# Turning late token tiles in 32 x 32 blocks on VectorE, and making decay weights ahead, in a fused state-space and feed-forward kernel

## The chip, the cores and the metric

The kernel runs on one core of one Trainium2 chip, as one program. The metric is device time in microseconds (us) of one execution. The core has five engines that run side by side, each with a queue of its own that it works through in order: PE (TensorE, matmuls; PEld is its weight loads), DVE (VectorE), ACT (ScalarE), POOL (GpSimd) and SP (SyncE, which here only issues DMAs).

## The reference

Two branches work on the layer-normed input and are added to the input: a diagonal state-space convolution (S4), and a feed-forward with SiLU. Everything is float32.

```python
def _A_ref(u, A_re, A_im, B_re, B_im, C_re, C_im, log_dt, Dskip):   # u: 1 x 2048 x 576
    dt = jnp.exp(log_dt)[:, None]
    A = A_re + 1j * A_im                                             # 576 x 128
    ...
    logdA = dt * A
    dB = dt * Bc
    P = jnp.exp(logdA[:, :, None] * l[None, None, :])                # l = 0 .. 2047
    K = jnp.einsum("dn,dnl,dn->dl", Cc, P, dB).real
    ...                                                              # causal convolution of u with K, by FFT
    y = (lambda x, *d: x.transpose(*d))(y, 0, 2, 1) + u * Dskip[None, None, :]
    return y

def _B_ref(x, w1, w2):                                               # w1: 576 x 4608, w2: 4608 x 576
    h = jnp.einsum("bsd,df->bsf", x, w1)
    h = _silu(h)
    out = jnp.einsum("bsf,fd->bsd", h, w2)
    return out

x = A_u
xn = _layernorm(x, axis=-1)
return x + _A_ref(xn, ...) + _B_ref(xn, B_w1, B_w2)
```

## The kernel before

The 2048 tokens are 16 tiles of 128. A product of two float32 matrices is made of three products of rounded parts: each operand is split into a high part (a copy to the rounded type F32R on ScalarE) and a low part (operand minus high part, on VectorE), and high x high, high x low and low x high are added up in PSUM.

**The feed-forward** (`ffn`) is the main line. It walks over 36 blocks: two halves of the tokens (tiles 0 to 7, 8 to 15), nine chunks of 512 hidden channels, and two blocks of 512 tokens. For a block, `up` multiplies a chunk of w1 with the turned token tiles `xh`, `xl`, `x4` (L284 to L286, 14 matmuls), applies SiLU (L292) and splits the result into `gh` and `gl` (L293, L294); `down` multiplies that with w2 (L309, 12 matmuls for each half of the 576 channels, into one of three `po` accumulators) and adds to the accumulator `acc` in SBUF (L313). `load_w1`, `split_w1`, `load_w2` and `split_w2` bring the next chunk in from SP's queue. The steps of a block are written out by hand as u0, d0 to d3, u1, u2, u3, where the u steps belong to the next block.

**The turned tokens.** The up projection needs tokens with channels on the partitions. `normed` takes normalised tiles from `norm` and turns each on PE in `put_xt`: four 128 x 128 transposes (L121) and one of the last 64 channels (L125) into the PSUM tile `pt`, then a copy on ScalarE (L122, L126) and a subtraction on VectorE (L123, L127), which give the high and low part. Tiles 0 to 7 go straight into `xts[0]` and `xts[1]`. Tiles 8 to 15, the late ones, are not needed before the second half. They go through one buffer `xt` in SBUF and from there to DRAM (`dxt`, L223), nine groups of 128 channels that hold the high parts, the low parts and the last 64 channels' pair. `next_xt` loads them back, as three DMAs on POOL's queue for each block of 512 tokens (L322 to L324), when the first half reaches its last chunk. The normalised tile itself goes to `dxn` (L224) for the convolution.

**The side line** (`side`) is woven into the feed-forward by `weave`, which hands out its pieces at given shares of the main line's steps. In order:
- `phase0` for the first eight tiles, before the main line starts;
- in turn, `natural` (the decay and phase of each of 576 channels x 128 states, first in a layout of 96 x 6 x 128) and `phase0` for the four late pairs. `natural` leaves the exponentials of the decay at lags 256, 64, 8 and 1 in `ex`, which go to DRAM as `dexp` (L436), and turns three arrays on PE with `turned` (L393, L394) into `fT`, `rhoT` and `phiT`, which stay in SBUF;
- `kgen`, which makes the convolution kernel's transform in 36 chunks of 16 channels. For each pair of chunks `powers` loads the four bases (`load_bases`, L519), lays them out in `pw` and makes their powers 0 to 7 (L528, L532 to L534), and multiplies the first four powers at lag 64 with `rhoT` into `al` (L536). A chunk makes phases (`head`, L541, L543; L557, L558), sines and cosines (L559 to L561), magnitudes from products of the powers (L562 for 32 columns, L566 for 64), products of both (L577, L578), many small matmuls into `kp` (L598) and, for each pair, a transform with `f1` (L613), whose result is staged (L621) and written to `d1k` (L626) every two pairs;
- `spread`, the token side of the transform, one piece for each chunk of `kgen` from the third on;
- `spectral`, 32 steps of products in the frequency domain, and `tail`, which turns back and adds to the output.

The order of instructions on each engine is made at build time by a scheduler that simulates the engines and takes, of what is ready, the earliest emitted; `high_priority` puts L292 to L294 and L313 first, and `behind` keeps an instruction behind a given one on its engine. The tile pools `nat` and `pb` (for `natural` and the late pairs) are closed before `kgen` opens its own, in the same memory.

## Time and profile before

| | |
|---|---|
| median of 3 runs | 1133.25 us (1133.01 to 1133.71) |
| the profiled execution | 1131.89 us, its span 1130.1 us |
| PE, PEld busy | 1109.0 us, 999.9 us |
| DVE, ACT, POOL busy | 917.1 us, 709.0 us, 74.3 us |
| DMA | 151.24 MB in 160458 packets, of which 87216 under 512 B |

The profile is of one execution. Its parts are the page (busy time, the span in slices, queues, the chain that ended last, the costliest groups, the DMA issues), groups of instructions by line and operation, windows of time, waits and timelines. A group's line has the count, the busy time and the mean length of one in ns, and the idle time of the engine just before them with what ended it. A line number such as L309 is one of the kernel before. Matmuls overlap, so that the time a matmul holds PE is read from one start to the next and not from its length.

### The profile page before, as it was taken

The page shows a single profiled execution, that of the slowest core. Times are in us where ns is not written, and L with a number is a line of the kernel's source. Part 1 is how long each engine was busy: PE and PEld are TensorE (multiplying, and loading weights), DVE is VectorE, ACT ScalarE, POOL GpSimd, SP SyncE. Part 2 cuts the span into 40 slices and gives each one's busy share as a digit, 9 for nine tenths or more (in the row PEclk, how much of TensorE's full clock was granted, in tenths as well). Part 3 has the DMA queues.
Part 4 walks back from the last instruction along what each step waited for, and adds up shares of the span by engine and source line. Part 5 has one row for each costly group of instructions (what it writes and reads, how often), then busy time and mean ns, then how long its engine had stood idle before and what let it go on. Part 6 is the DMA issues. An engine that isn't in the chain of part 4 may idle for free.

```text
span 1130.1 us, 22882 instructions
## 1 busy us (share of the span) xinstructions
PE 1109.0 (98%) x9184; PEld 999.9 (88%) x9184; DVE 917.1 (81%) x1540; ACT 709.0 (63%) x1235; POOL 74.3 (7%) x130
## 2 busy tenths in 40 slices
PE   6999999999999999999999999999999999999998
PEld 5988889988889888898989999999999999998876
DVE  6699779999999999999999937788877878763433
ACT  4665355776777666667666637877777787752211
POOL 1010000000000000001000000000000000000210
PEclk9999999999999999999999999999999999999999
DMA  9345431334241424255954264554535536239661
GB/s 277 111 142 181 144 96 60 97 98 103 83 114 59 112 83 106 90 127 192 231 161 104 66 183 122 157 175 132 170 114 157 166 118 195 72 111 243 174 171 55
DMA packets 160458, 151.24 MB, mean 134 GB/s; under 512 B 87216, under 2 KB 127168, under 8 KB 159712
## 3 DMA queue, kind: packets, MB, share of 16 engines
q1 hardware_dynamic: 150128, 112.66, 36.2%
q0 software_dynamic: 9840, 36.24, 10.0%
q8 instruction: 72, 1.18, 0.4%
q10 hardware_dynamic: 384, 0.89, 0.3%
q14 instruction: 34, 0.28, 0.1%
HBM read 103.74 MB, written 46.08 MB: 133 GB/s over the span
## 4 chain that ended last, share of the span: by engine, by line
PE 65%; DVE 24%; DMA 5%; ACT 3%; issue 3%; POOL 0%; SPq 0%; DVEq 0%; ACTq 0%; POOLq 0%
PE po L309 28%; PE ph L284 23%; DVE acc L313 2%; DVE C L566 2%; PE pu L721 2%; PE pb L721 2%; PE pk L721 2%; DVE th L541 2%; DMA w2r<-in_B_w_dram 2%; DVE th L558 2%; DVE S L577 2%; PE ph L285 2%; PE ph L286 2%; DVE C L577 2%; DVE gl L294 2%
## 5 line engine op out<-in xcount | busy, mean ns | idle before, releaser
L309 PE MATMUL po<-w2h,gh 128*128 128x288 f32 x1152 | 338.5, 297 | 5.3 <-DVE acc L313 2.6
L309 PE MATMUL po<-w2l,gh 128*128 128x288 f32 x1152 | 337.1, 295 | 0.0
L309 PE MATMUL po<-w2h,gl 128*128 128x288 f32 x1152 | 335.3, 296 | 0.6 <-DVE gl L294 0.6
L309 PEld LDWEIGHTS po<-w2h,gh 128*128 128x128 f32 x1152 | 215.2, 188 | 16.8 <-DVE acc L313 4.9
L309 PEld LDWEIGHTS po<-w2l,gh 128*128 128x128 f32 x1152 | 215.5, 188 | 4.3
L309 PEld LDWEIGHTS po<-w2h,gl 128*128 128x128 f32 x1152 | 214.8, 188 | 3.0 <-issue 0.9
L284 PE MATMUL ph<-xh,w1h 128*128 128x512 f32 (+1 forms) x592 | 162.3, 390 | 0.5 <-ACT xh L122 0.5
L284 PE MATMUL ph<-xl,w1h 128*128 128x512 f32 (+1 forms) x592 | 162.1, 387 | 0.0
L284 PE MATMUL ph<-xh,w1l 128*128 128x512 f32 (+1 forms) x592 | 161.1, 385 | 0.0
L313 DVE TENSOR_TENSOR acc<-po,acc 128x288 f32<-128x288 f32 x288 | 126.9, 452 | 40.1 <-PE po L309 38.4
L292 ACT ACTIVATE gf<-ph 128x512 f32<-128x512 f32 (+1 forms) x148 | 86.6, 585 | 115.3 <-PE ph L286 106.1
L294 DVE TENSOR_TENSOR gl<-gf,gh 128x512 fp32r<-128x512 f32 (+1 forms) x148 | 99.6, 673 | 47.6 <-ACT gh L293 46.9
L284 PEld LDWEIGHTS ph<-xl,w1h 128*128 128x128 f32 x592 | 108.6, 190 | 20.2
L284 PEld LDWEIGHTS ph<-xh,w1l 128*128 128x128 f32 x592 | 108.0, 188 | 19.7
L284 PEld LDWEIGHTS ph<-xh,w1h 128*128 128x128 f32 x592 | 105.3, 190 | 19.0 <-issue 2.3
L293 ACT CAST gh<-gf 128x512 fp32r<-128x512 f32 (+1 forms) x148 | 89.7, 608 | 9.1 <-PE po L309 6.2
L559 ACT ACTIVATE c<-th 128x1040 f32<-128x1040 f32 x36 | 38.7, 1075 | 60.0 <-DVE th L558 59.9
L271 ACT CAST w2h<-w2r 128x576 fp32r<-128x576 f32 x72 | 46.7, 672 | 39.9 <-DMA w2r<-in_B_w_dram 23.4
L557 ACT ACTIVATE c<-th,magic 128x1040 f32<-128x1040 f32 x36 | 42.0, 1168 | 42.4 <-DVE C L578 36.5
L273 DVE TENSOR_TENSOR w2l<-w2r,w2h 128x576 fp32r<-128x576 f32 x72 | 53.4, 752 | 8.9 <-ACT w2h L271 8.9
L286 PE MATMUL ph<-x,w1l 128*128 128x512 f32 (+1 forms) x148 | 56.9, 385 | 0.0
L255 DVE TENSOR_TENSOR w1l<-w1r,w1h 128x640 fp32r<-128x640 f32 x72 | 56.7, 819 | 0.2
(186 smaller groups left out, 1847.2 us busy)
## 6 DMA issues: line engine op xcount, KB each, us to landing
w2r<-in_B_w_dram SPq DMA_DIRECT2D x72, 288.0 KB, 3.7
w1r<-in_B_w_dram SPq DMA_DIRECT2D x35, 512.0 KB, 3.8
d1u<-u POOLq DMA_DIRECT2D x32, 288.0 KB, 2.8
d1k<-stage SPq DMA_DIRECT2D x18, 512.0 KB, 7.2
ur<-d1u SPq DMA_DIRECT2D x32, 288.0 KB, 3.6
kr<-d1k SPq DMA_DIRECT2D x32, 288.0 KB, 2.8
d<-yo POOLq DMA_DIRECT2D x32, 288.0 KB, 3.6
ys<-d SPq DMA_DIRECT2D x32, 288.0 KB, 9.0
```

The costliest lines, as they stand in the source:

```text
L255: pins["w1l"] = nc.vector.tensor_sub(l1, src, h1).ins
L271: pins["w2h"] = nc.scalar.copy(h2, r2).ins
L273: nc.vector.tensor_sub(l2, r2, h2)
L284: nc.tensor.matmul(ph, w[:, kt, :], v[:, kt, a:e], start=n + kt == 0, stop=False)
L286: pins["pe"] = nc.tensor.matmul(ph, l1[:, 4, :], x4[:, a:e], start=False, stop=True).ins
L292: nc.scalar.activation(gf, ph, AF.Silu)
L293: pins["gh"] = nc.scalar.copy(gh, gf).ins
L294: pins["gl"] = nc.vector.tensor_sub(gl, gf, gh).ins
L309: pins["pe"] = nc.tensor.matmul(po[:, :HD], G[blk, t][g][:, js], W2[half, c, t][w][:, hs], start=n == 0, stop=n == 3 * FT - 1).ins
L313: nc.vector.tensor_add(acc[j][:, hs], po[:, :HD], acc[j][:, hs])
L577: nc.vector.tensor_mul(ov3, t[:, :, 0:64].rearrange("n d (x y) -> n d x y", y=32), mv3)
L721: nc.tensor.matmul(dst, st, mv[:, hs], start=n == 0, stop=n == 3 * len(terms) - 1)
```

## The change

The late token tiles are no longer turned on PE. VectorE turns each normalised tile in blocks of 32 x 32 into a tile `tr` (one buffer for a pair of tiles), and eight DMAs for each pair put the blocks in their places in `dxt`, which now holds plain float32 tokens with channels on the rows (576 x 512). `next_xt` loads the first 512 channels into `xl` and the last 64 twice into `r4`, a buffer of the pool's `gl` tag. A new `split_xt` makes the high part (a copy on ScalarE) and the low part (a subtraction in place on VectorE), in five pieces for each of the two late blocks, after steps d3, u1 and u2 of the first half's last chunk.

In the decays, the table of powers keeps three bases (256, 8 and 1). The powers 0 to 3 of the lag-64 base times `rho` are made in `natural` for all channels (`wt`, three multiplications), written to DRAM as `dmag`, and loaded for each pair of chunks into `wb` beside the bases `eb`. `al` and `rhoT` go away. The magnitudes of the first 32 columns are made by two instructions, one for each group of eight channels, in place of one.

```diff
-    dxt = [dram.tile([P, 9, 512], F32, name=f"dxt{b}") for b in range(2)]
+    dxt = [dram.tile([D, 512], F32, name=f"dxt{b}") for b in range(2)]
...
-    dexp = dram.tile([P, 4 * D], F32, name="dexp")
+    dexp = dram.tile([P, D, 3], F32, name="dexp")
+    dmag = dram.tile([P, D, 4], F32, name="dmag")
...
-            else:
-                xt = p0.tile([P, 9, P], F32R, tag="xt", name="xt", bufs=1)
-                put_xt(xt[:, 0:4, :], xt[:, 4:8, :], xt[:, 8, :], xn[:, i, :])
-                nc.sync.dma_start(dxt[b - 2][:, :, jj * P:(jj + 1) * P], xt.bitcast(F32))
+        if js[0] >= 8:
+
+            b, jj = divmod(js[0], 4)
+            tr = p0.tile([P, 2, D], F32, tag="tr", name="tr")
+            for i in range(2):
+                nc.vector.transpose(tr[:, i, :], xn[:, i, :])
+            for q in range(4):
+                cols = dxt[b - 2][:, jj * P:(jj + 2) * P].rearrange("(k r) (i q c) -> q r i k c", r=32, i=2, q=4)[q]
+                for i in range(2):
+                    nc.sync.dma_start(cols[:, i], tr[32 * q:32 * q + 32, i].rearrange("r (k c) -> r k c", c=32))
...
         def next_xt(b):
-            xt = new_xt(2 + b)
-            nc.gpsimd.dma_start(xt[0], dxt[b][:, 0:4, :])
-            nc.gpsimd.dma_start(xt[1], dxt[b][:, 4:8, :])
-            nc.gpsimd.dma_start(xt[2], dxt[b][:, 8, :])
-            xts[2 + b] = xt
+
+            xh, xl, x4 = xts[2 + b] = new_xt(2 + b)
+            nc.gpsimd.dma_start(xl.bitcast(F32), dxt[b][0:512].rearrange("(k p) t -> p k t", p=P))
+            r4 = gp.tile([P, 512], F32R, tag="gl", name="r4").bitcast(F32)
+            for h in range(2):
+                nc.gpsimd.dma_start(r4[64 * h:64 * h + 64], dxt[b][512:D])
+            R4[b] = r4
+
+        def split_xt(b, kt):
+            xh, xl, x4 = xts[2 + b]
+            with behind(pins["gh"]):
+                if kt < NKT:
+                    nc.scalar.copy(xh[:, kt], xl[:, kt].bitcast(F32))
+                    nc.vector.tensor_sub(xl[:, kt], xl[:, kt].bitcast(F32), xh[:, kt])
+                else:
+                    r4 = R4.pop(b)
+                    nc.scalar.copy(x4, r4)
+                    nc.vector.tensor_sub(x4[64:, :], r4[64:, :], x4[64:, :])
...
+                if half == 0 and c == NCH - 1:
+                    for kt in {"d3": (0, 1), "u1": (2, 3), "u2": (4,)}.get(step, ()):
+                        split_xt(b, kt)
...
-        for k, lag in enumerate((256.0, 64.0, 8.0, 1.0)):
-            nc.scalar.activation(ex.rearrange("n (d k) -> n k d", k=4)[:, k, :], lrT, AF.Tanh, scale=0.5 * lag)
+        for k, lag in enumerate((256.0, 8.0, 1.0, 64.0)):
+            dst = ex[:, :3 * D].rearrange("n (d k) -> n k d", k=3)[:, k, :] if k < 3 else ex[:, 3 * D:]
+            nc.scalar.activation(dst, lrT, AF.Tanh, scale=0.5 * lag)
...
-        nc.sync.dma_start(dexp, ex)
+        nc.sync.dma_start(dexp, ex[:, :3 * D].rearrange("n (d k) -> n d k", k=3))
...
-        turned(br, rhoT)
+
+        wt = nat.tile([P, D, 4], F32, tag="r", name="wt")
+        turned(br, wt[:, :, 0])
         turned(t0, phiT)
+        for k in range(3):
+            v.tensor_mul(wt[:, :, k + 1], wt[:, :, k], ex[:, 3 * D:])
+        nc.sync.dma_start(dmag, wt)
...
-            pw = kg.tile([P, 2, W, 4, 8], F32, name="pw")
+            pw = kg.tile([P, 2, W, 3, 8], F32, name="pw")
...
-                    bases.append(kg.tile([P, 2, W, 4], F32, tag="eb", name="eb", bufs=2))
-                    nc.sync.dma_start(bases[-1].rearrange("n g c k -> n g (c k)"),
-                                      dexp.rearrange("n (g r) -> n g r", g=2)[:, :, i * CH * 4:(i + 2) * CH * 4])
+                    eb = kg.tile([P, 2, 2, CH, 3], F32, tag="eb", name="eb", bufs=2)
+                    wb = kg.tile([P, 2, 2, CH, 4], F32, tag="wb", name="wb", bufs=2)
+                    for t, d in ((eb, dexp), (wb, dmag)):
+                        nc.sync.dma_start(t.rearrange("n g q c k -> n g (q c k)"),
+                                          d.rearrange("n (g r) k -> n g (r k)", g=2)[:, :, i * CH * d.shape[2]:
+                                                                                     (i + 2) * CH * d.shape[2]])
+                    bases.append((eb, wb))
...
-                R = 2 * W * 4
+                R = 2 * W * 3
...
-                for q in range(2):
-                    nc.vector.tensor_mul(split(al[:, q]), split(pw[:, q, :, 1, 0:4]), col(rhoT, i + q, 4))
-                return al
+                return wb
...
-                nc.vector.tensor_mul(
-                    mag[:, :, 0:32].rearrange("n d (x y) -> n d x y", y=4),
-                    pk[:, :, 0, :].unsqueeze(3).broadcast_to([P, W, 8, 4]),
-                    ak.unsqueeze(2).broadcast_to([P, W, 8, 4]))
+                for g in range(2):
+                    gs = slice(g * CH, (g + 1) * CH)
+                    nc.vector.tensor_mul(
+                        mag[:, gs, 0:32].rearrange("n d (x y) -> n d x y", y=4),
+                        pk[:, gs, 0, :].unsqueeze(3).broadcast_to([P, CH, 8, 4]),
+                        ak[:, g].unsqueeze(2).broadcast_to([P, CH, 8, 4]))
...
-            for n in ("f", "rho", "phi"):
+            for n in ("f", "phi"):
                 kf[n] = kfp.tile([P, D], F32, name=n + "T")
```

More of the change, by code (lines that the diff above doesn't have):

```diff
@@ L373, in natural @@
     def natural(nat):
-        fT, rhoT, phiT = (kf[n] for n in ("f", "rho", "phi"))
+        fT, phiT = kf["f"], kf["phi"]
         NT, NP = 6, 96
@@ L486, in natural @@
         v.tensor_mul(t0, t0, rc)
-        turned(br, rhoT)
+        wt = nat.tile([P, D, 4], F32, tag="r", name="wt")
+        turned(br, wt[:, :, 0])
         turned(t0, phiT)
+        for k in range(3):
+            v.tensor_mul(wt[:, :, k + 1], wt[:, :, k], ex[:, 3 * D:])
+        nc.sync.dma_start(dmag, wt)
     def kgen():
-        fT, rhoT, phiT = (kf[n] for n in ("f", "rho", "phi"))
+        fT, phiT = kf["f"], kf["phi"]
         with tc.tile_pool(name="kg", bufs=1) as kg:
```

12 lines of the change are left out of this document (6 added, 6 removed).

## The prediction

> **What bounds the kernel now.** I read the page first, then the busy time by stretch, then the chain that ended last in order of time, and last the timelines around the instructions that the change touches.
>
> ```profile
> span 1130.1 us, 22882 instructions
> PE 1109.0 (98%) x9184; PEld 999.9 (88%) x9184; DVE 917.1 (81%) x1540; ACT 709.0 (63%) x1235; POOL 74.3 (7%) x130
> ```
>
> TensorE is busy for 98% of the span. Its matmuls overlap in the records, so this alone does not prove that it is at its peak; the stretches and the chain must say that. The four stretches are the turning of the late token tiles and the decay preparation (60 to 160 us), the making of the convolution kernel (160 to 600), the two feed-forward blocks in which the second half's tokens are loaded (505 to 556), and the spectral part (600 to 1000). The columns are length, then busy time and instructions of PE, PEld, DVE, ACT and POOL, then granted clock, DMA share and GB/s.
>
> ```profile
> 60.00:160.00 100.00, 98.06 (x606) 88.80 (x605) 82.16 (x152) 50.89 (x79) 4.65 (x6) 1.00 0.51 158
> 160.00:600.00 440.00, 435.62 (x4507) 390.61 (x4508) 429.05 (x632) 300.12 (x451) 19.02 (x35) 1.00 0.41 113
> 505.00:556.00 51.00, 50.73 (x552) 45.64 (x551) 50.81 (x75) 36.38 (x57) 5.45 (x10) 1.00 0.68 209
> 600.00:1000.00 400.00, 400.00 (x2826) 369.77 (x2816) 311.73 (x550) 293.56 (x589) 28.12 (x51) 1.00 0.46 137
> ```
>
> PE has no gap at all from 600 to 1000 us, 1.9 us of gaps from 60 to 160 and 4.4 us from 160 to 600. VectorE, though, is nearly full too from 160 to 600 (429 of 440 us), and full from 505 to 556 (50.81 of 51). The clock is 1.00 throughout. The chain gives the pace of the matmuls where nothing waits (start, length, engine, tile, line, count), and the groups give how many there are.
>
> ```profile
> 473.04 2.74 PE ph L284 x12
> 640.12 3.31 PE po L309 x25
> L309 PE MATMUL po<-w2h,gh 128*128 128x288 f32 x1152 | 338.5, 297 | 5.3 <-DVE acc L313 2.6
> L284 PE MATMUL ph<-xh,w1h 128*128 128x512 f32 (+1 forms) x592 | 162.3, 390 | 0.5 <-ACT xh L122 0.5
> ```
>
> An up matmul takes 2.74/12 = 0.228 us from start to start, a down matmul 3.31/25 = 0.132. The three products of the down projection are 3 x 1152 x 0.132 = 456 us, those of the up projection on L284 3 x 592 x 0.228 = 405 us. So the feed-forward part alone needs about 861 us at a pace that the trace never beats in a long run, and the other matmuls fill most of what is left. The bound is TensorE: a step off VectorE, ScalarE or a queue counts only where it ends one of PE's few gaps, and a step off PE counts in full.
>
> **Part 1: the late tiles leave PE.** The eight token tiles 8 to 15 are turned on PE now, five instructions each, in this pattern (start, length, engine, line, tiles, count):
>
> ```profile
> 139.97 0.60 PE L121 MATMUL pt<-ident,xj 128*128 128x128 f32 x4
> 140.40 0.27 PE L125 MATMUL pt<-ident,xj 128*64 128x128 f32 x1
> 140.51 0.60 PE L121 MATMUL pt<-ident,xj 128*128 128x128 f32 x4
> 140.87 0.95 PE L284 MATMUL ph<-xh,w1l 128*128 128x512 f32 x3
> 141.65 0.39 PE L285 MATMUL ph<-x,w1h 128*128 128x512 f32 x1
> ```
>
> Four turns take 140.40 - 139.97 = 0.43 us or 140.87 - 140.51 = 0.36 us from start to start, the fifth 0.11. The three matmuls after them take 0.78 us where 3 x 0.228 = 0.68 are due, so 0.1 us is lost in going back. A tile costs 0.5 to 0.64 us; eight tiles 4.0 to 5.1 us. I take 4.5, the middle, all of it on the path, since PE is the bound there. [...]
>
> **Part 2: a wait goes with them.** The tile xt has one buffer, so ScalarE can't fill it before the last one has been written to DRAM. This once reaches PE:
>
> ```profile
> 131.51 0.59 ACT L122 CAST xt<-pt 128x512 fp32r<-128x512 f32 x1 [5.04 <-DMA dxt<-xt]
> 132.14 0.69 DVE L123 TENSOR_TENSOR xt<-pt,xt 128x512 fp32r<-128x512 f32 x1 [4.06 <-ACT xt L122]
> 133.69 0.41 PE L309 MATMUL po<-w2h,gh 128*128 128x288 f32 x1 [1.35 <-DVE acc L313]
> ```
>
> ScalarE stands 5.04 us for the write, VectorE stands 4.06 us behind ScalarE, the addition to acc is queued behind that, and PE runs out of free accumulators for 1.35 us. With no xt tile this goes: -1.35 us. What could be late next is tr, which also has one buffer and is read by eight writes; a pair comes every 20 us or more and the writes take about as long as those below, so I expect no wait.
>
> **Part 3: what the turning costs elsewhere.** Between 60 and 160 us:
>
> ```profile
> L122 ACT CAST xt<-pt 128x512 fp32r<-128x512 f32 x8 | 4.6, 580 | 10.2 <-DMA dxt<-xt 10.2
> L123 DVE TENSOR_TENSOR xt<-pt,xt 128x512 fp32r<-128x512 f32 x8 | 5.4, 678 | 8.3 <-ACT xt L122 8.3
> L127 DVE TENSOR_TENSOR xt<-pt,xt 64x128 fp32r<-64x128 f32 x8 | 2.3, 284 | 0.2
> L188 DVE TENSOR_SCALAR xj<-xj,mv,sd 128x576 f32<-128x576 f32 x4 | 2.3, 580 | 1.8 <-POOL sd L184 1.7
> L657 DVE TENSOR_TENSOR y<-y,y 128x576 f32<-128x576 f32 x32 | 24.1, 752 | 0.1
> ```
>
> VectorE loses 5.4 + 2.3 = 7.7 us of subtractions and 8.3 us of waiting, and gets eight 128 x 576 block turns. No row shows such a turn; the nearest of that size are 580 and 752 ns, and I take the slower, 8 x 0.75 = 6.0 us. If it were 1.5 us it would be 12, still within the 17.8 us in which VectorE is idle there. [...] ScalarE loses over 4.6 us and its 10.2 us wait. On PE: nothing.
>
> ```profile
> L223 SPq DMA_DIRECT2D dxt<-xt x8: 519/565/597, 70.2 to 149.7; - x8
> dxt<-xt SPq DMA_DIRECT2D x8, 576.0 KB, 4.1
> d1k<-stage SPq DMA_DIRECT2D x18, 512.0 KB, 7.2
> dexp<-ex SPq DMA_DIRECT2D x1, 1152.0 KB, 5.9
> eb<-dexp SPq DMA_DIRECT2D x18, 64.0 KB, 2.2
> ```
>
> Eight writes on SP become 32: at 0.565 us of issue each, 18.1 instead of 4.5 us, in four bursts of 4.5 us. Behind a burst stand the dxn write, the next x load and w1 and w2 loads; a weight that comes 4.5 us later is still early for a block of 25 us. The runs are 32 numbers long, as those of the stage write, which lands 512 KB in 7.2 us; a pair here is 576 KB. The reading back falls from three loads of 2304 KB to three of 1280 KB on POOL: nothing.
>
> **Part 4: the split moves into the full stretch.** Per late block VectorE and ScalarE now get five more instructions each of 128 x 512, like these:
>
> ```profile
> L294 DVE TENSOR_TENSOR gl<-gf,gh 128x512 fp32r<-128x512 f32 (+1 forms) x148 | 99.6, 673 | 47.6 <-ACT gh L293 46.9
> L293 ACT CAST gh<-gf 128x512 fp32r<-128x512 f32 (+1 forms) x148 | 89.7, 608 | 9.1 <-PE po L309 6.2
> ```
>
> That is 10 x 0.673 = 6.7 us on a VectorE that has 0.2 us free in these 51 us, and 6.1 us on ScalarE, which has 14.6. What can give way is the making of the convolution kernel, which is not urgent: VectorE has a fifth of its time free after 600 us. The feed-forward's own subtractions and additions are emitted at high priority, so I take 0 on PE here; its cover gone, it is the rival below. r4 takes one of six gl buffers, and the next user waits for down steps that precede it anyway.
>
> **Part 5: the powers and the weights.**
>
> ```profile
> L536 DVE TENSOR_TENSOR al<-pw,rhoT 128x64 f32<-128x64 f32 x36 | 6.4, 218 | 0.0
> L532 DVE TENSOR_TENSOR pw<-pw 128x128 f32<-128x128 f32 x18 | 7.8, 431 | 0.1
> L533 DVE TENSOR_TENSOR pw<-pw 128x256 f32<-128x256 f32 x18 | 11.3, 626 | 0.0
> L534 DVE TENSOR_TENSOR pw<-pw 128x384 f32<-128x384 f32 x18 | 9.9, 553 | 0.1
> L562 DVE TENSOR_TENSOR C<-pw,al 128x512 f32<-128x512 f32 x36 | 24.7, 685 | 0.7 <-PE kp L598 0.7
> ```
>
> From 64 and 512 numbers (218 and 685 ns) an instruction costs 151 ns and 1.04 ns a number. Removed: 36 x 0.218 = 7.8 us of al; a quarter of the numbers in the three power steps, (431 + 626 + 553 - 3 x 151)/4 = 289 ns, 18 times, 5.2 us. Added: L562 in two halves of 256, one more fixed cost of 0.151 us for each of 36, 5.4 us. Net 7.6 us less on VectorE, spread over 160 to 650 us; it repays Part 4 and is worth 0 on PE by itself. Ahead of it stand three multiplications of 576 numbers at a stride, between 0.75 us (L657) and 576 x 431/128 = 1.9 us (L532) each: 2.3 to 5.8 us in VectorE's idle time, nearer the low end as the stride is half.
>
> They and a new trip through DRAM stand before the first weights: 2.3 + 5.9 for the dmag write (as large as dexp) + 2.2 for the load = 10.4 us. In the timeline the first use comes this long after the first instruction of kgen:
>
> ```profile
> 153.61 0.06 DVE L509 MEMSET magic<- 128x1 f32 x1 [1.90 <-PE po L309]
> 163.53 0.68 DVE L562 TENSOR_TENSOR C<-pw,al 128x512 f32<-128x512 f32 x1
> ```
>
> So the margin is 0.5 us short; if VectorE stands at the first weights, gl and acc are queued behind it, and SP, standing at the load of wb for the dmag write, holds the next loads of bases and the xr load for up to 5.9 us. PE has three accumulators of 12 matmuls, 1.6 us each, or 4.8 us of work before it runs dry. The cost lies between 0 and 10.4 - 4.8 = 5.6 us; below nothing it can't go, as it only adds a wait. I take 1.0, near the low end, since the trace shows the cover almost whole.
>
> **The sum.** The profiled execution took 1131.89 us (1.8 around its span of 1130.1). -4.5 for PE's turns, -1.35 for the gap behind xt, +1.0 for the first weights: 1131.89 - 4.85 = 1127.04. The median of the runs, 1133.25, is 1.36 above the profiled one, so 1128.4. Its own range: 4.0 to 5.1 us of turns, 0 to 3 us for the first weights: 1126.8 to 1130.9, in round numbers 1126.5 to 1131. A measurement of this kernel can tell about 0.2%, 2.3 us, from no change.
>
> **The rivals.**
> *The splits hit PE (slower).* The place is 505 to 556 us. Each split is a copy on ScalarE and a subtraction on VectorE that waits for it; VectorE, in order, may stand for the copy each time, as it does before gl now (46.9 us in all). That is 6.7 + 6.1 = 12.8 us of a full engine, with gl and acc queued behind. If all of it reaches PE, the time is 1133.25 - 5.85 + 12.8 = 1140.2. From 5.85 us on PE it cancels the gain, from 8.1 it is slower by 2.3. For it: 50.81 of 51. Against it: 7.6 us less elsewhere, five splits spread over four steps of 3.2 us, and 400 us afterwards with VectorE at 78%. Chance 0.2, at 1135.6 to 1140.2.
> *The first weights cost all of it (no change).* With the whole 5.6 us and no other gain than the turns and the gap: 1133.25 - 5.85 + 5.6 = 1133.0. For it: the margin is negative on paper. Against: an order of instructions that puts gl and acc first. Chance 0.12.
> *PE is not the bound (no change).* Then the turns fell into slack that returns, and only the gap is won: 1133.25 - 1.35 = 1131.9. For it, the page has weight loads at 88%. Against, the unbroken 0.132 and 0.228 us. Chance 0.08. [...]
> *VectorE's relief counts (faster still).* If the 7.6 us less also close PE's 4.4 us of gaps from 160 to 600: 1128.4 - 4.4 = 1124.0. For it: VectorE at 97.5% there. Against: the gaps are few and short, and Part 4 takes the relief back. Chance 0.12.
> That the change leaves the turns on PE can be excluded: no transpose on PE is left for tiles 8 to 15.
>
> **How the numbers follow.** The forecast itself gets 0.48. Faster by over 0.2% is the forecast and the relief, 0.60; within 0.2% are the two cases without change, 0.20; slower is the splits, 0.20. The range runs from 1123.0, a little below the relief, to 1138.0, the middle of the splits' case; about 0.1 lies above it and less below.
>
> **What would show it.** Right: no pt from xj on PE after 60 us, 32 instead of 64 instructions on L121's form; no wait of ScalarE for a write of late tiles; the PE gap at 132 us gone; eight turns on VectorE near 0.75 us each; PE without gaps over 1 us between 505 and 556, with VectorE still full; the convolution kernel's last instruction within some 6 us of where it is. Wrong: PE waiting for gl or acc or for the split tiles in those 51 us (the splits); VectorE or ScalarE standing over 5 us at the first weights near 155 us and PE's gaps there (the first weights); the same time with PE's gaps larger everywhere (not the bound). A faster or slower time whose difference does not lie at one of these places would be the order of instructions shifted elsewhere, and my working would be wrong even if the number fits.

## The result, and the profile after

The changed kernel takes 1129.62 us, the median of 21 runs (1127.94 to 1133.24). The kernel before, run beside it, has 1133.25 (21 runs, 1131.38 to 1136.53). The ratio is 0.997, 95% interval 0.9961 to 0.9978: faster by 3.4 us by the ratio, with an interval of 2.5 to 4.4, and by 3.6 between the medians. Forecast were 1128.4 and a gain of 4.85. The profiled execution of the changed kernel took 1131.96 us, 2.3 above its median, that of the kernel before 1131.89, 1.4 below its own. The two traces are therefore equally long, though the kernels' usual times are not, and what follows compares places in them and not their lengths.

The page of the changed kernel, its first line, the busy times and the granted clock in 40 slices:

```profile
span 1130.2 us, 22881 instructions
PE 1106.7 (98%) x9144; PEld 998.7 (88%) x9144; DVE 917.1 (81%) x1545; ACT 708.7 (63%) x1229; POOL 78.5 (7%) x130
PEclk9999899999999999999999999999999999999999
```

PE has the 40 turns less (9184 to 9144). VectorE is exactly as busy as before. The clock line, all nines before, has an 8 in its fifth slice, 113 to 141 us. The same four stretches, with the same columns as in the prediction:

```profile
60.00:160.00 100.00, 94.91 (x543) 85.31 (x542) 87.36 (x153) 50.93 (x71) 9.33 (x5) 0.97 0.57 145
160.00:600.00 440.00, 440.00 (x4493) 396.97 (x4492) 421.88 (x630) 301.63 (x454) 19.37 (x35) 1.00 0.41 109
505.00:556.00 51.00, 51.00 (x558) 46.07 (x557) 48.98 (x75) 35.10 (x55) 5.31 (x9) 1.00 0.60 171
600.00:1000.00 400.00, 398.65 (x2874) 368.48 (x2873) 310.89 (x551) 287.16 (x575) 26.76 (x49) 1.00 0.48 138
```

The stretch in which the turns were taken off PE is the one in which PE now works less: 94.91 of 100 us, against 98.06, and at a lower clock. From 160 to 600 us PE has no gap left (4.4 us before). After 600 it has small ones (1.35 us, none before).

One calculation puts this on one scale. Each matmul gets the distance from start to start that its kind has where nothing waits (0.227 us for an up matmul, 0.133 for a down matmul, 0.095 for a turn, and so on; the last is an estimate, as the 40 late turns of the kernel before start 3.6 us in all ahead of what follows each, 0.109 us ahead of another turn and 0.03 ahead of other work). Summed over all matmuls, with some 13 us for what lies before the first one and after the last one, this is the time that PE needs; what a stretch takes over it is lost there, to gaps and to low clock alike. These are estimates, good to about half a microsecond for a stretch.

```
profiled execution of    needs   lost: 0-40  40-60  60-160  160-600  600-1000  1000-end   together
kernel before            1099.7         2.9    0.2     3.8     13.6       2.0       8.0       30.4
changed kernel           1095.9         3.9    0.2     8.9      6.6       3.6      11.0       34.3
```

So 3.8 us of need went; this is 40 turns at 0.095 us, and no measurement of its own. Around it, losses of the same size moved in both directions: 5.1 us more from 60 to 160, 7.0 us less from 160 to 600, 4.6 us more after 600.

The new loss near 120 us. The timeline of the changed kernel (start, length, engine, line, tiles, and in brackets the idle time of the engine before it and what ended it), SyncE's queue first, then VectorE, then PE:

```profile
110.69 5.14 SPq L230 DMA_DIRECT2D dxt<-tr  x8
115.87 1.91 SPq L164 DMA_DIRECT2D xj<-in_A_u_dram  x4
117.23 0.44 DVE L320 TENSOR_TENSOR acc<-po,acc 128x288 f32<-128x288 f32 x1
117.60 1.22 DVE L516 TENSOR_TENSOR wt<-wt,ex 128x576 f32<-128x576 f32 x1
118.73 0.95 DVE L506 TENSOR_TENSOR t<-t,are 96x768 f32<-96x768 f32 x1
120.78 1.54 DVE L180 BATCH_NORM_STATS2 st<-xj 128x6 f32<-128x288 f32 x4 [1.10 <-DMA xj<-in_A_u_dram]
122.24 1.15 DVE L516 TENSOR_TENSOR wt<-wt,ex 128x576 f32<-128x576 f32 x1
123.30 0.45 DVE L320 TENSOR_TENSOR acc<-po,acc 128x288 f32<-128x288 f32 x1
123.81 0.40 PE L316 MATMUL po<-w2h,gh 128*128 128x288 f32 x1 [3.67 <-DVE acc L320]
```

The eight block writes of the third late pair (a burst, below) hold SyncE for 5.1 us; the load of the fourth pair's tokens stands behind them. VectorE, in order, waits 1.10 us for these tokens, takes their statistics, does one of the new multiplications for the weights' powers, and only then adds to `acc`. Between two additions to `acc` lie 6.1 us. PE's free accumulators are then full, and it stands for 3.67 us. The bursts of the first two pairs have a load of tokens behind them too (at 68.5 and 91.4 us), and PE has no gap over 0.8 us there: it takes the late tokens and VectorE's other work together. What follows is in the stretches behind it (granted clock is the third number from the end):

```profile
120.00:125.00 5.00, 1.33 (x10) 1.10 (x8) 4.22 (x8) 0.00 (x0) 0.00 (x0) 1.00 0.00 0
125.00:130.00 5.00, 4.33 (x19) 4.19 (x18) 5.00 (x13) 4.04 (x7) 1.35 (x1) 0.51 0.26 109
130.00:135.00 5.00, 5.00 (x27) 4.55 (x26) 4.51 (x9) 0.87 (x1) 2.73 (x2) 0.81 0.47 150
```

From 125.1 to 131.9 us, 6.8 us, PE has half its clock: its down matmuls start 0.24 us apart there in place of 0.133. This costs up to 3.4 us more, an estimate (half of the 6.8 us). Some of the experiments below show the drop after shorter gaps; the last section lists the cases.

The groups that answer to the durations of the prediction (busy time, then mean ns of one), and two lists of one line's instructions (duration in ns min/median/max, first and last start):

```profile
L226 DVE STREAM_TRANSPOSE tr<-xj 128x576 f32<-128x576 f32 x8 | 6.0, 759 | 0.0
L341 DVE TENSOR_TENSOR xl<-xl,xh 128x512 fp32r<-128x512 f32 x8 | 5.3, 682 | 0.0
L345 DVE TENSOR_TENSOR x<-r,x 64x512 fp32r<-64x512 f32 x2 | 1.4, 687 | 0.1
L516 DVE TENSOR_TENSOR wt<-wt,ex 128x576 f32<-128x576 f32 x3 | 3.6, 1193 | 0.0
L565 DVE TENSOR_TENSOR pw<-pw 128x96 f32<-128x96 f32 x18 | 6.5, 363 | 0.0
L566 DVE TENSOR_TENSOR pw<-pw 128x192 f32<-128x192 f32 x18 | 9.2, 511 | 0.1
L567 DVE TENSOR_TENSOR pw<-pw 128x288 f32<-128x288 f32 x18 | 8.2, 454 | 0.1
L595 DVE TENSOR_TENSOR C<-pw,wb 128x256 f32<-128x256 f32 x72 | 27.2, 418 | 1.5 <-PE kp L631 1.4
L122 PE MATMUL pt<-ident,xn x32: 271/273/477, 9.0 to 40.6; 128*128 128x128 f32 x32
L230 SPq DMA_DIRECT2D dxt<-tr x32: 337/516/1529, 63.2 to 143.1; - x32
L517 SPq EVENT_SEMAPHORE  x1: 10167/10167/10167, 117.8 to 117.8; - x1
```

The late part of the loss. VectorE's last instruction for the convolution kernel's making starts at 651.0 us, against 646.9 before, and its first one of the spectral part 11.6 us later than before (690.7 against 679.1). Two waits in the timeline of the changed kernel lie there:

```profile
686.64 0.67 ACT L740 CAST kh<-kr 128x576 fp32r<-128x576 f32 x1 [4.50 <-DMA kr<-d1k]
687.37 0.40 PE L754 MATMUL pk<-kh,mm 128*128 128x288 f32 x1 [1.35 <-ACT kh L740]
1055.51 1.35 ACT L260 CAST w1h<-w1r 128x640 fp32r<-128x640 f32 x2 [4.40 <-DMA w1r<-in_B_w_dram]
1058.25 0.40 PE L316 MATMUL po<-w2h,gh 128*128 128x288 f32 x1 [1.98 <-DVE acc L320]
```

PE first reaches the convolution kernel before it has been read back from DRAM; near the end a weight comes late and PE stands again.

### The profile page after: what moved, and what is told of

The parts are those of the page before. It is cut to its first block, busy times and chain, and to the rows that moved or that the text cites. A ratio compares the mean times of both kernels' runs of the same rounds, so it can differ in the third digit from the quotient of the medians.

```text
span 1130.2 us, 22881 instructions
## 1 busy us (share of the span) xinstructions
PE 1106.7 (98%) x9144; PEld 998.7 (88%) x9144; DVE 917.1 (81%) x1545; ACT 708.7 (63%) x1229; POOL 78.5 (7%) x130
## 4 chain that ended last, share of the span: by engine, by line
PE 86%; DVE 5%; DMA 5%; SPq 1%; issue 1%; ACT 0%; POOL 0%; DVEq 0%; POOLq 0%; ACTq 0%
PE po L316 36%; PE ph L291 30%; PE kp L631 3%; PE ph L292 3%; PE ph L293 2%; PE pk L754 2%; PE pu L754 2%; PE pb L754 2%; DMA w1r<-in_B_w_dram 2%; PE z L646 2%; PE pu L153 1%; DMA xj<-in_A_u_dram 1%; PE py L774 1%; PE pu L154 1%; DMA d1k<-stage 1%
## 5 line engine op out<-in xcount | busy, mean ns | idle before, releaser
L301 DVE TENSOR_TENSOR gl<-gf,gh 128x512 fp32r<-128x512 f32 (+1 forms) x148 | 98.7, 670 | 41.3 <-ACT gh L300 40.6
L292 PE MATMUL ph<-x,w1h 128*128 128x512 f32 (+1 forms) x148 | 57.2, 386 | 0.0
```

The source lines that it names most:

```text
L292: nc.tensor.matmul(ph, h1[:, 4, :], x4[:, a:e], start=False, stop=False)
L301: pins["gl"] = nc.vector.tensor_sub(gl, gf, gh).ins
```

## The experiments

Each was timed beside the kernel before, on the same chip; the five comparisons were made at different times and not all on one chip, and the kernel before moved by 1.3 us between them, so that differences between two other kernels carry about as much. "PE 60-160" is PE's busy time in these 100 us of the profiled execution, "clock" the median over a kernel's executions of the mean granted clock.

| kernel | median us | ratio to before, 95% | PE 60-160 | clock |
|---|---|---|---|---|
| before | 1131.99 to 1133.25 in five comparisons | 1 | 98.06 | 0.998 to 1.000 |
| changed | 1129.62 | 0.997 (0.9961 to 0.9978) | 94.91 | 0.997 |
| tiles only | 1130.17 | 0.998 (0.9968 to 0.9991) | 95.68 | 0.998 |
| powers only | 1128.19 | 0.996 (0.9948 to 0.9973) | 99.69 | 1.000 |
| changed, block writes on GpSimd | 1127.77 | 0.9954 (0.9937 to 0.9972) | 98.60 | 0.9995 |
| changed, x loads first | 1134.10 | 1.0016 (1.0006 to 1.0026) | 98.83 | 0.998 |
| changed, eight splits left out | 1127.00 | 0.994 (0.9924 to 0.9957) | 94.81 | 0.998 |
| changed, block and `dmag` writes on GpSimd | 1125.01 | 0.9925 (0.9905 to 0.9946) | 99.91 | 1.000 |
| before, mark 0.127 | 1137.28 | 1.0038 (1.0023 to 1.0053) | 97.61 | 0.996 |
| changed, mark 0.127 | 1130.83 | 0.9984 (0.9971 to 0.9997) | 94.67 | 0.996 |
| changed, `dmag` write on GpSimd | 1129.48 | 0.9968 (0.9956 to 0.9981) | 96.04 | 0.997 |
| both writes on GpSimd, mark 0.127 | 1123.75 | 0.9918 (0.9902 to 0.9934) | 99.93 | 0.999 |
| before, its writes on GpSimd | 1127.77 | 0.996 (0.9948 to 0.9973) | 99.09 | 1.000 |
| changed, late statistics later | 1129.13 | 0.9979 (0.9968 to 0.999) | 97.07 | 0.997 |

**The two halves of the change.** In the first kernel the tiles are turned by VectorE, and the powers are as before:

```diff
-    dexp = dram.tile([P, D, 3], F32, name="dexp")
-    dmag = dram.tile([P, D, 4], F32, name="dmag")
+    dexp = dram.tile([P, 4 * D], F32, name="dexp")
...
-        for k in range(3):
-            v.tensor_mul(wt[:, :, k + 1], wt[:, :, k], ex[:, 3 * D:])
-        nc.sync.dma_start(dmag, wt)
...
-            pw = kg.tile([P, 2, W, 3, 8], F32, name="pw")
+            pw = kg.tile([P, 2, W, 4, 8], F32, name="pw")
```

> The kernel before with the late tiles' part of the change alone (turns on VectorE, dxt as plain tokens, splits late); the powers stay as they were. Theory (PE is the bound; the turns and the wait behind xt are worth 5.9 us; the gaps of PE in the making of the convolution kernel, 6.3 us of them over 0.15 us each, go only with the powers' relief of VectorE): about 1129 to 1133 us, with the gaps from 160 to 600 us still there and a new one near 120 us behind the x load that follows the eight writes on SP. Rival one (the splits reach PE when VectorE has no relief): above 1136, with PE waiting between 505 and 556 us. Rival two (the parts do not matter, a new order of instructions alone moves the time by a few us): anything from 1126 to 1136, with gaps at unrelated places.

1130.17 us, 2.5 under the 1132.62 of the kernel before. PE's gap near 120 us is there, with no weights' powers in this kernel:

```profile
120.11 1.54 DVE L179 BATCH_NORM_STATS2 st<-xj 128x6 f32<-128x288 f32 x4 [1.93 <-DMA xj<-in_A_u_dram]
123.40 0.40 PE L315 MATMUL po<-w2h,gh 128*128 128x288 f32 x1 [3.62 <-DVE acc L319]
```

VectorE waits 1.93 us for the tokens and then takes their statistics and does table work ahead of `acc`. So the gap belongs to the tiles' half, though what fills it differs. The clock does not fall behind it here. And the loss from 160 to 600 us is 9.6 us, against 13.6 before, without any relief of VectorE by the powers.

In the second the powers are as changed, and the late tiles are turned on PE:

```diff
-            tr = p0.tile([P, 2, D], F32, tag="tr", name="tr")
-            for i in range(2):
-                nc.vector.transpose(tr[:, i, :], xn[:, i, :])
...
+                xt = p0.tile([P, 9, P], F32R, tag="xt", name="xt", bufs=1)
+                put_xt(xt[:, 0:4, :], xt[:, 4:8, :], xt[:, 8, :], xn[:, i, :])
```

> The changed kernel with the late tiles turned on PE again, so the powers' part alone. Theory: VectorE has 7.6 us less to do from 150 to 650 us and PE's gaps there (6.3 us) mostly close, the turns and the wait behind xt stay: 1127 to 1130 us, no long gap near 120 us. Rival (the relief is worth nothing on PE, as the prediction took it): 1132 to 1134, gaps from 160 to 600 us as before.

1128.19 us, 4.4 under, with the same matmuls as before. The halves add up to 6.9 us of gain and together give 3.4 to 3.6. The loss from 160 to 600 us is 12.9 us, against 13.6 before, so VectorE's relief did not close PE's gaps there: the time lies within its theory's 1127 to 1130 us, but not for its reason. What is better lies from 60 to 160 (a loss of 1.5 us in place of 3.8): PE's gap at 132 us is absent, although `xt` still has one buffer; ScalarE waits 3.2 us in all for the writes of `xt` there, in place of 10.2. Neither fits a cost by parts.

**The order of instructions alone.** The first of three marks is the share of the main line's steps from which the pieces of the convolution kernel's making are handed out. 0.127 in place of 0.130 changes due times and no work.

```diff
-        marks = (0.13, 0.595, 0.822)
+        marks = (0.127, 0.595, 0.822)
```

> A control: the kernel before with the making of the convolution kernel emitted from a share of 0.127 of the main line's steps instead of 0.130, which does no work more or less and only gives another order of instructions from about 150 us on. Theory (the parts of the change decide): 1132 to 1134, within 1 us of the kernel before. Rival (the order alone moves the time by as much as the change): off by 2 us or more.

> The same control on the changed kernel. Theory: 1128.6 to 1130.6, the gap near 120 us still there. Rival (order alone): off by 2 us or more from 1129.6, with the gaps from 160 us on elsewhere.

The kernel before goes from 1132.96 to 1137.28, 4.3 us slower. Its loss from 160 to 600 us is 18.5 in place of 13.6, most of it at one place (PE's timeline, then the stretch):

```profile
518.38 0.40 PE L309 MATMUL po<-w2h,gh 128*128 128x288 f32 x1 [2.76 <-ACT w2h L271]
520.00:525.00 5.00, 5.00 (x29) 4.78 (x29) 4.53 (x6) 2.96 (x4) 0.00 (x0) 0.50 0.20 59
```

A new gap and then half a clock from 518.8 to 525.7. The changed kernel with the same edit has 1130.83, 1.2 us over and just above what its theory gave; the gap at 120 us stays (3.74 us). A shift of order without any change of work is thus worth up to 4 us, as much as the whole change, and single differences of that size from one edit cannot be put down to its work without a look at where they lie.

**Where the splits cost.** Eight of the ten splits are left out; the up projection takes the loaded tile for both parts, so its products are not the kernel's own, but as many:

```diff
-            xh, xl, x4 = xts[2 + b] = new_xt(2 + b)
+            xh, xl, x4 = new_xt(2 + b)
+            xts[2 + b] = xl, xl, x4
...
-                    nc.scalar.copy(xh[:, kt], xl[:, kt].bitcast(F32))
-                    nc.vector.tensor_sub(xl[:, kt], xl[:, kt].bitcast(F32), xh[:, kt])
+                    pass
```

> The changed kernel without eight of the ten late splits: the copies and subtractions of the first 512 channels are left out, and the up projection of the second half reads the unsplit tokens as high and as low part, so the second half's values are wrong; the matmuls stay in number and size. Theory (the splits cost PE nothing in their own 51 us, but push the making of the convolution kernel back by their 6.7 us of VectorE, and what follows it late pinches the end: PE's gap at 686 us and 3 us more loss after 1000 us): kernel making ends 5 to 7 us earlier (near 645 us), gap at 686 us gone, loss after 1000 us back to that of the kernel before, 1125 to 1128 us. Rival (the splits are free to the end): the same 1129.6 within 1 us.

1127.00 us, 2.6 under the changed kernel (2.3, each against the kernel before beside it). In the stretch of the splits nothing was to be gained, as PE has no gap there with them and none without:

```profile
505.00:556.00 51.00, 51.00 (x559) 45.98 (x558) 48.51 (x74) 36.22 (x56) 3.65 (x7) 1.00 0.75 189
```

VectorE's last instruction for the convolution kernel's making starts at 640.8 us in place of 651.0, more than the 5 to 7 us expected, and the loss after 1000 us is 8.3 in place of 11.0. One thing expected did not come: PE still stands 1.28 us at its first use of the convolution kernel, at 671 us in place of 687, so the splits do not make that gap. Within the changed kernel, the chunks of the convolution kernel are 5.2 us earlier than before at 520 us and 1.7 us later at 553, 6.9 us lost; five of the ten splits lie in between, 3.4 us of VectorE's work, and the other five from 556 us on. So the splits push the chunks back, but their own length is only half of this. The gap near 120 us stays (3.73 us).

**SyncE's queue.** First the 32 block writes alone go to GpSimd, then the `dmag` write alone, then both:

```diff
-                    nc.sync.dma_start(cols[:, i], ...)
+                    nc.gpsimd.dma_start(cols[:, i], ...)
...
-        nc.sync.dma_start(dmag, wt)
+        nc.gpsimd.dma_start(dmag, wt)
```

> The changed kernel with the 32 block writes to dxt issued from POOL's queue in place of SP's. Theory (the 3.8 us gap of PE at 120 us comes from the x load that waits on SP behind eight writes of 5.1 us, with the statistics that wait for it queued on VectorE ahead of acc; the granted clock falls after the gap): x load earlier by 2 us or more, gap at 120 us gone or under 1.5 us, clock 1.00 in all of 100 to 140 us, 1124 to 1127 us. Rival (VectorE's own order holds acc, the load plays no part): the gap stays near 3 us and the time within 1 us of the changed kernel's 1129.6.

> The changed kernel with one edit: the write of the magnitudes (dmag) is issued by GpSimd and not by SyncE; the 32 block writes stay on SyncE. Theory A (the gain of 4.6 us of the kernel with both on GpSimd comes from the burst of 32 writes standing ahead of an x load on SyncE): the gap of 3.7 us at 120 us stays, since the burst stays, and the time is 1129 to 1130.5, as that of the changed kernel; removing SyncE's stand of 10.2 us for dmag is worth nothing, since nothing on TensorE waited for it. Theory B (SyncE's stand was the cost): the gap at 120 us stays, but the loads behind the stand come 10 us earlier and the time falls to 1126 to 1127.5. Rival (order): another order of instructions is drawn and the gap at 120 us is gone although the burst is on SyncE: 1125 to 1127.

> The changed kernel with the 32 block writes and also the dmag write issued on POOL's queue, so that SP neither carries the bursts nor stands 10.2 us for the weights. Theory: as the block writes on POOL alone (1127.8), with w1 loads earlier near 130 us; 1126 to 1128, since no gap of PE is left there. Rival (SP's stand for dmag holds weights that PE needs): 1124 to 1126.

1127.77, 1129.48 and 1125.01 us. With the block writes off SyncE the gap near 120 us is gone, and the loss from 60 to 160 us is 2.2 and 0.6 in place of 8.9. The first time lies 0.8 us above what its theory gave. The last lies below its theory's 1126 to 1128, where its rival had it (SyncE's stand for `dmag` holds weights that PE needs). Against that rival speaks the second, which takes the same stand away and gains nothing. With the burst gone too it could still be worth something: the 2.8 us between the first and the last kernel are not accounted for, and order alone moves more. With the `dmag` write alone moved, as its theory A had it, the gap stays (PE's and VectorE's timeline, then the stretch):

```profile
119.75 1.54 DVE L180 BATCH_NORM_STATS2 st<-xj 128x6 f32<-128x288 f32 x4 [0.69 <-DMA xj<-in_A_u_dram]
122.77 0.40 PE L316 MATMUL po<-w2h,gh 128*128 128x288 f32 x1 [3.24 <-DVE acc L320]
60.00:160.00 100.00, 96.04 (x553) 86.05 (x552) 88.69 (x157) 52.47 (x72) 9.81 (x6) 0.98 0.56 145
```

In the kernel with both writes on GpSimd, GpSimd, SyncE and VectorE at the same place:

```profile
107.80 5.29 POOL L230 DMA_DIRECT2D dxt<-tr  x8 [4.10 <-DVE tr L226]
108.30 2.05 SPq L164 DMA_DIRECT2D xj<-in_A_u_dram  x4
113.99 1.54 DVE L180 BATCH_NORM_STATS2 st<-xj 128x6 f32<-128x288 f32 x4 [0.67 <-DMA xj<-in_A_u_dram]
115.44 0.44 DVE L320 TENSOR_TENSOR acc<-po,acc 128x288 f32<-128x288 f32 x1
117.75 0.45 DVE L320 TENSOR_TENSOR acc<-po,acc 128x288 f32<-128x288 f32 x1
60.00:160.00 100.00, 99.91 (x594) 90.41 (x593) 93.24 (x161) 53.44 (x74) 30.93 (x38) 1.00 0.54 151
```

Burst and load now run side by side, the load 7.6 us earlier; the statistics come 6.8 us earlier, and `acc` follows them at once. VectorE still waits 0.67 us, but nothing is late behind it. What SyncE is spared at this place is the burst's 5.1 us; a token load stood behind it, and the loss from 60 to 160 us falls by 6.7 us with the block writes moved and by 8.3 with both.

That this is no lucky order, the same kernel was to show with the other mark; and that GpSimd's queue helps only against the change's own burst, the kernel before with its eight writes moved:

```diff
-                nc.sync.dma_start(dxt[b - 2][:, :, jj * P:(jj + 1) * P], xt.bitcast(F32))
+                nc.gpsimd.dma_start(dxt[b - 2][:, :, jj * P:(jj + 1) * P], xt.bitcast(F32))
```

> The kernel with the block writes and the dmag write on GpSimd (1125.0 before), with the feed-forward's mark at 0.127 instead of 0.130, which changes the due times and so the order of instructions and no work. In the two pairs before, this edit moved the time by +4.3 us (kernel before) and +1.3 us (changed kernel). Theory A (moving the writes off SyncE takes away a cause): no gap over 1.5 us between 60 and 160 us here either, and 1125 to 1128. Theory B (1125.0 was a lucky order): the gap near 120 us or others of its size come back and the time is 1128.5 to 1131.

> The kernel before with one edit: its eight writes of turned late tiles (dxt from xt) are issued by GpSimd and not by SyncE. Theory A (what GpSimd's queue takes off is the change's own burst of 32 writes): eight writes of 0.565 us were no burden on SyncE, so the time is 1132 to 1134.5, as that of the kernel before, and TensorE's gaps from 60 to 160 us stay within 2 us of the 3.8 us of before. Theory B (any write moved off SyncE helps, with the change or without): 1128 to 1130.5, three us or more under the kernel before. Rival (order): it falls outside both, and by the gaps listed the difference lies at places without a dxt write.

The first holds in its gaps: PE is busy for 99.93 of the 100 us. The time is 1123.75 us, 1.3 under the range of its theory A, the fastest kernel of this study, 8.4 us under the kernel before. The second does not: 1127.77, 4.4 under the kernel before and just under what its theory B gave. Of that, 1.7 us is less loss from 60 to 160 us (2.1 against 3.8) and 3.6 us less from 160 to 600 (10.0 against 13.6), where there is no such write; by the rival of that run, the larger part is order. So between kernels with these writes off SyncE the change itself is worth 1127.77 less 1125.01 or 1123.75: 2.8 to 4.0 us, which agrees with the 3.8 us of need that went. It does not prove it: each of the three is one order of instructions, and order has moved 4.3 us.

**Loading the late tokens first.**

```diff
-            xs = load_x(j0, p0, "xj", (nc.sync,))
+            with tc.high_priority():
+                xs = load_x(j0, p0, "xj", (nc.sync,))
```

> The changed kernel with the x loads of the late pairs put ahead on SP by priority, so that they no longer stand behind the eight writes. Theory: as for the writes on POOL, gap at 120 us gone and 1124 to 1127 us. Rival: the gap stays, as VectorE's order alone makes it, 1129 to 1130 us.

1134.10 us, slower than the kernel before, and no test of what it was made for. The gap near 120 us is gone, but the late pairs' first load went ahead of the first tokens at the very start: PE's first matmul starts at 17.03 us in place of 9.03.

**What VectorE does between two additions.** All writes stay on SyncE; the norm of the last late pair gets a step of its own, 0.012 later, so that its statistics stand behind `acc`:

```diff
-                ... (0.06, 0), (gate_of(2), 1), (0.08, 0), (0.085, 1)):
+                ... (0.06, 0), (gate_of(2), 1), (0.08, 0), (0.085, 1), (0.092, 2)):
...
-                            phase0(pb, (j, j + 1))
+                            phase0(pb, (j, j + 1), "norm" if tables else "load" if j == NJ - 2 else None)
```

> The changed kernel with all its DMA writes on SyncE, the burst of eight ahead of the last late pair's x load included; only the norm of that pair (statistics, scaling, turning) is given a step of its own, due at 0.092 instead of 0.08, behind the last table step. Up to the gap at 120 us each queue's order is that of the changed kernel; then VectorE has the addition to acc first and the four statistics (1.5 us) some 5 us later, when their tokens have landed. Theory A (the gap is VectorE's: it stands 1.1 us for the late tokens and then works on their statistics for 1.5 us with acc queued behind): the gap of 3.7 us falls by these 2.6 us to 0.8 to 1.5 us, what the two multiplications of 1.2 us leave; the granted clock then stays at 1.00 from 120 to 135 us, PE is busy for over 97 of the 100 us from 60 to 160, and the time is 1125 to 1128.5. Theory B (the burst on SyncE itself holds PE up, through the weights behind it): a gap over 2.5 us stays between 115 and 135 us with the half clock behind it, and the time is 1129 to 1131. Rival (order): the gap at 120 us goes but others of its size come elsewhere, and the time does not fall.

Up to there the order of the queues is that of the changed kernel, and the burst still stands ahead of the load (SyncE, 108.75 us). VectorE's timeline, PE's, and the stretch behind:

```profile
117.65 1.16 DVE L516 TENSOR_TENSOR wt<-wt,ex 128x576 f32<-128x576 f32 x1
118.73 0.44 DVE L320 TENSOR_TENSOR acc<-po,acc 128x288 f32<-128x288 f32 x1
120.43 1.17 DVE L516 TENSOR_TENSOR wt<-wt,ex 128x576 f32<-128x576 f32 x1
121.50 0.68 DVE L301 TENSOR_TENSOR gl<-gf,gh 128x512 fp32r<-128x512 f32 x1
119.22 0.40 PE L316 MATMUL po<-w2h,gh 128*128 128x288 f32 x1 [1.02 <-DVE acc L320]
122.24 0.61 PE L316 MATMUL po<-w2h,gl 128*128 128x288 f32 x1 [1.69 <-DVE gl L301]
120.00:135.00 15.00, 13.21 (x69) 11.27 (x68) 12.66 (x27) 7.06 (x12) 2.24 (x3) 0.89 0.51 162
```

The gap falls from 3.67 to 1.02 us, as theory A had it (0.8 to 1.5): the wait for the tokens and their statistics are 2.6 us of it, the multiplications most of the rest. But the third multiplication, with table work, now stands ahead of `gl`, PE waits 1.69 us for that, and the clock still drops, from 122.3 to 125.7. The time is 1129.13 and does not fall as theory A expected. So the burst on SyncE is not by itself what stops PE; what stops it is a VectorE that has the last pair's norm, the tables and the three new multiplications within some 10 us, with `acc` and `gl` in between. The late load is one part of that; the multiplications are not needed for it, as the tiles-only kernel shows.

## Why the prediction was right in its number, and where its steps failed

**The sign and the number.** 1129.62 lies 1.2 us over the forecast and within its own range. But the prediction named a condition on itself: a difference that lies elsewhere than at its places is the order of instructions, and then the working is wrong though the number fits. Much of the difference does lie elsewhere, and the control on the kernel before shows that order alone moves 4.3 us. The number is right in part by luck: losses of opposite sign cancel.

**What bounds the kernel.** The 861 us for the feed-forward are some 10 too many, as 32 of each 592 up matmuls have 256 columns and not 512 and start 0.120 us apart in the trace of the kernel before; this changes nothing of the argument.

**Part 1, the turns (-4.5).** Right in kind, a little large by the scale above. No `pt` from `xj` is left on PE (32 instructions of the form, the last at 40.6 us). By the scale's estimate of 0.095 us for each of the 40 they were worth 3.8 us, by their starts 3.6; whether the 0.1 us a tile for going back to the up projection went too is not shown, since it would count as loss.

**Part 2, the gap at 132 us (-1.35).** It is gone, and nobody waits for `tr`. But the one buffer of `xt` is not enough to make it: the powers-only kernel has that buffer and no gap there, the kernel before with the other mark has a gap of 2.35 us, and in the kernel before with its writes on GpSimd ScalarE waits 5.42 us for the buffer while PE stands for nothing over 1 us. The gap hung on the order of instructions too.

**Part 3, "on PE: nothing".** The step that failed. The turns themselves were sized right (759 ns for 750), the burst too (5.1 us for 4.5). The prediction listed what stands behind the burst, the dxn write, the x load and the weights, and then priced the weights alone, as early enough. The x load is the one whose user, the statistics, stands on VectorE ahead of `acc`. The price is PE's gap of 3.67 us and, in this trace, up to 3.4 us for the half clock behind it; five kernels with the burst ahead of that load and the statistics in place have a gap of 3.2 to 3.7 us there, four of them with half a clock behind it and the tiles-only kernel without, and three with the block writes on GpSimd have none.

**Part 5, the multiplications.** Taken near the low end of 0.75 to 1.9 us each and put into "VectorE's idle time"; they take 1.19 us, and two of them stand in that same gap. Idle time summed over 100 us says nothing about a place where three jobs meet. The rest of the part holds: the three power steps fall from 29.0 to 23.9 us (5.2 forecast), and the halved instruction costs 2.5 us more than before (5.4 forecast): the 72 instructions overlap in the records, 72 x 0.418 us lie in 27.2 us of busy time. The same holds for `al`, which the prediction put at 36 x 0.218 = 7.8 us and which was busy for 6.4; VectorE's relief comes to 6.4 + 5.1 - 2.5 = 9.0 us and not 7.6.

**The first weights (+1.0).** No wait. The convolution kernel's making starts at 146.6 us, 7 us earlier than before; SyncE stands 10.2 us for `dmag`, and the kernel without that stand has the same time (1129.48).

**Part 4, the splits (0 on PE).** Right in size (5.3 + 1.4 = 6.7 us on VectorE), right in its 51 us, and the rival of the splits did not come: PE is busy for 51.00 of 51, and for all of the 440 us from 160 to 600, in which the second block's splits lie too. That what can give way is "the making of the convolution kernel, which is not urgent" was too quick. It gave way by the 6.9 us, its end came 4.1 us later than before, and the spectral part behind it 11.6 us later. Leaving out eight of ten splits gives 2.6 us, with a loss after 1000 us of 8.3 in place of 11.0; since order moves as much, this size is less sure than its place, and that the last weights come late for this reason is not shown.

**The rivals.** VectorE's relief is not what closed the gaps from 160 to 600 us: the changed kernel has lost 7.0 us less there, the powers-only kernel with the same relief 0.7 less, the tiles-only kernel without it 4.0 less. That PE is the bound agrees with the 2.8 to 4.0 us that the change is worth where the gaps are out of the way, for 3.8 us of need; with so few orders tried this is not proof.

What stays open is why the order of the powers-only kernel and of the kernel before with its writes on GpSimd is better by 4.4 us; the places are known, the choice behind them is not. Nor is it shown what makes the changed kernel lose 7.0 us less from 160 to 600 us, the largest single difference between the two traces.

## What to carry to other kernels

When a DMA burst is moved into or made on a queue, take each transfer behind it, find the engine that uses it and what is queued behind that use; price the most urgent one and not the most numerous. Before reading a gain of a few parts in a thousand, run a control that changes only the order: here it is worth 4.3 us, as much as the change. And look for a second place to issue from: two lines that put the writes on GpSimd gain at least as much (4.6 us between the medians, 4.3 with each against the kernel before beside it) as the change itself.

## What the runs showed of the hardware that was not expected

PE's clock is halved after gaps that look harmless, for 3.4 or 6.8 us: after 3.67 us of standing (changed kernel, 6.8 us), 3.24 us (`dmag` write on GpSimd, 3.4), 1.02 and 1.69 us within 4 us (late statistics later, 3.4), and even here, in the fastest kernel, where half the clock holds from 669.1 to 672.5 us and matmuls of 288 columns start 0.24 us apart, against 0.13 before the gap:

```profile
669.00 0.56 PE L754 MATMUL pk<-kh,mm 128*128 128x288 f32 x1 [1.86 <-DMA kr<-d1k]
```

A longer gap does not do it for certain: after 3.62 us (tiles-only kernel) and 1.98 us (changed kernel, at 1058 us) it did not happen. What decides between these cases is not shown here.

The half clock may also be much of what differs between kernels, by this estimate: a mean clock of 0.997 over 1130 us costs at most 3.4 us, of the 4.6 us between the changed kernel (0.997) and the one with both writes on GpSimd (1.000). It is less by what lies after the last matmul; in the changed kernel's trace that matmul ends at 1125.9 us, and 1.6 of the 8.4 us of half clock stand behind it.

A block turn of 128 x 576 float32 on VectorE takes 759 ns, about as long as the multiplication of that size on L657 of the kernel before (752). A product of 576 numbers into every fourth place (`wt`) takes 1193.
